# Splitting the last stage of an inverse FFT by residues modulo 3: three full matmuls and vector sums in place of four matmuls on 96 rows

## The chip, the cores and the metric

One Trainium2 chip, one of its cores. The metric is the device time of one execution in microseconds (us), lower is better.

## What is computed

Three parts follow one another on an input of 8 batches, 3072 tokens and 256 channels, all in 32-bit floats:

```python
X = np.fft.rfft(x, axis=1)
y = np.fft.irfft(X * (filt_r + 1j * filt_i), n=3072, axis=1)     # filter along the tokens
xk = mu_k * y + (1 - mu_k) * y_prev                              # y_prev: y one token earlier
xr = mu_r * y + (1 - mu_r) * y_prev
z = sigmoid(xr @ w_r) * (np.maximum(xk @ w_k, 0) ** 2 @ w_v)     # 256 -> 1024 -> 256
h = np.maximum(np.maximum(z @ w1, z @ w2), z @ w3)               # 256 -> 768
out = h @ w_out                                                  # 768 -> 256
```

## The kernel before, in words

The 3072 tokens of a batch are written as 96 x 32: token 32 p + m. The forward and the inverse FFT both run as matmuls with small tables. `fft` (L400) emits, per batch, the forward steps, the product with the filter and the first inverse step (`c_mm`, L506); its results go to a tensor in DRAM, `s2`, with the axes m (32), r (4 real components), g (24 frequency groups) and the channels. `fft_first` (L531) does the same for batch 0.

The second inverse step is the place of the change. A tile is four values of m (`MC`) with all 96 values of p, so 384 tokens; eight tiles make a batch, 64 make the run. `y_load` (L683) reads a tile's part of `s2` into `cin`, with the 96 pairs (r, g) on the partitions, by one DMA on SyncE's queue; the first tile of a batch also reads the last m into `cprev`. `y_mm` (L694) then does, for each half of the channels:

```python
for m in range(MC):
    mm(p[:, m], t[:, m, h * P : (h + 1) * P], wi_s[:, 0], m == 0, True, True)
...
nc.scalar.copy(yt[:, h, :, 1:], p[:, :MC].rearrange("c m t -> c t m"))
```

Each of the four matmuls has `cin` as the stationary operand (96 rows, 128 columns) and the 96 x 96 table `wi_s` as the moving one, in full 32-bit floats. ScalarE copies the 384 results out of PSUM into `yt`, where each p holds five tokens: the four of the tile and the one ahead of them, which GpSimd copies from the previous tile (L706), or ScalarE from `cprev` (L703). From `yt`, ScalarE (L714) and VectorE (L715) form the mixed input `xm`, and `split` (L249) makes a high part on ScalarE and a low part on GpSimd, `xh` and `xl`, once for r and once for k.

`r_mm`, `k_mm` and `v_mm` (L724, L734, L747) are the second part of the computation, with three matmuls for each product (high by high, high by low, low by high). A `v_mm` runs three `k_mm` later than the one whose result it uses (`LAG`, L208). `block` (L794), on pairs of tiles, is the third part, with `o_mm` (L865) behind it. Their weights `ws` are streamed from DRAM in the order of use, eight transfers ahead (`piece_of`, L333).

The order of the work is a list of units. For an even tile after the first ones, `y_mm` stands in the `kv` (L891) of the tile ahead of it, at its fifth `k_mm`; for an odd one, in `second` (L923), at the third block from its end. `drive` (L180) mixes the FFT of the next batch in between. A scheduler that works from estimated times then fixes the order on every engine, before the run; on the chip each engine's queue runs in that order.

Of the kernel before, what the change touches and what calls it, by code (L numbers as in the profile page):

```python
# [9 lines left out]
F32 = mybir.dt.float32  # L10
# [21 lines left out]
def fft_constants():  # L32


    n1 = np.arange(N1)
    n2 = np.arange(N2)
    wa = np.zeros((NP, 2, 2, NG))
    wi = np.zeros((2, 2, NG, NP))
    for j in range(2):
        for g in range(NG):  # L40
            ph = 2 * np.pi * ((n1 * g) % N1) / N1
            if g == 0:
                wa[j::2, 0, j, 0] = 1.0
                wa[j::2, 1, j, 0] = (-1.0) ** n1
                wi[0, j, 0, j::2] = 1.0 / N
                wi[1, j, 0, j::2] = (-1.0) ** n1 / N
            else:
                wa[j::2, 0, j, g] = np.cos(ph)
                wa[j::2, 1, j, g] = -np.sin(ph)
                wi[0, j, g, j::2] = 2 * np.cos(ph) / N  # L50
                wi[1, j, g, j::2] = -2 * np.sin(ph) / N
    wb = np.zeros((2, N2, NG, 2, N2))
    wc = np.zeros((2, N2, NG, 2, N2))
    freq = np.zeros((2, N2, NG), np.int64)
    for g in range(NG):
        for s in range(N2):
            if g:
                f = g + N1 * s
                th = 2 * np.pi * ((n2 * f) % N) / N
                c, sn = np.cos(th), np.sin(th)  # L60
                sg = 1.0 if s < NM else -1.0
                wb[0, :, g, 0, s] = c
                wb[1, :, g, 0, s] = sn
                wb[0, :, g, 1, s] = -sg * sn
                wb[1, :, g, 1, s] = sg * c
                wc[0, s, g, 0, :] = c
                wc[1, s, g, 0, :] = -sg * sn
                wc[0, s, g, 1, :] = sn
                wc[1, s, g, 1, :] = sg * c
                freq[:, s, g] = f if s < NM else N - f  # L70
            else:
                src = 0 if s < NM else 1
                f = N1 * s if s < NM else NG + N1 * (s - NM)
                th = 2 * np.pi * ((n2 * f) % N) / N
                c, sn = np.cos(th), np.sin(th)
                freq[:, s, g] = f
                if s == 0:
                    wb[0, :, 0, 0, 0] = 1.0
                    wb[0, :, 0, 1, 0] = (-1.0) ** n2
# [12 lines left out]
    return (
        wa.reshape(NP, NQ),
        wi.reshape(NQ, NP),
        wb.reshape(NK, NG, NK),
        wc.reshape(NK, NG, NK),
        freq.reshape(NK, NG),
    )


def radix3_constants():
# [62 lines left out]
    return w3, wb.reshape(NK, NG, NK)  # L164
# [33 lines left out]
def tile_spectral_moe(ctx: ExitStack, tc, x, xr, xz, filt, ones, wa, wa1, wi, wbc, wb1, wc1, filt1, filt0, mu, w_k, w_v, w_r, w1, w2, w3, w_out, out):  # L198
# [41 lines left out]
    wi_s = cpool.tile([NQ, 2, NP], F32, name="wi_s")  # L240
# [158 lines left out]

    def fft(b):  # L400
# [3 lines left out]
        s2 = dp.tile([NM, 4, NG, C], F32, tag="s2", name=f"s2_{b}")  # L404
        s2_of[b] = s2
# [100 lines left out]
        def c_mm(s):  # L506
# [6 lines left out]
            nc.scalar.dma_start(s2.rearrange("m r g c -> (m r) g c")[:, 2 * s : 2 * s + 2, :], o)  # L513
# [17 lines left out]
    def fft_first(pp, jobs):  # L531

        s1 = dp.tile([NM, 4, NG, C], F32, tag="s1", name="s1_0")
        s2 = dp.tile([NM, 4, NG, C], F32, tag="s2", name="s2_0")
        s2_of[0] = s2
# [96 lines left out]
        for s in range(NG // 2 + 2):  # L632
# [24 lines left out]
            if s >= 2:  # L657
# [6 lines left out]
                evac(s, p, s2.rearrange("m r g c -> (m r) g c")[:, 2 * s - 4 : 2 * s - 2, :], nc.scalar)  # L664
# [387 lines left out]
def layout(x, filt_r, filt_i, mu_k, mu_r, w_k, w_v, w_r, w1, w2, w3, w_out):  # L1052
    wa, wi, wb, wc, freq = fft_constants()
    C = x.shape[2]
    wa3, wb3 = radix3_constants()
    wah = np.stack(two_parts(wa3), axis=1)
    wis = np.zeros((NQ, 2, NP), np.float32)
    wis[:, 0] = wi
    wis[:, 1, 1:] = wi[:, :-1]
# [15 lines left out]
        "in_x": x[:1], "in_xr": xr, "in_xz": xz, "in_filt": filt, "in_ones": ones, "in_wa": wah, "in_wa1": wa.astype(np.float32), "in_wi": wis, "in_wbc": wbc, "in_wb1": wb.astype(np.float32), "in_wc1": wc.astype(np.float32),  # L1075
# [6 lines left out]
```

## Time and profile before

| | us |
|---|---|
| median of 3 runs (3162.06 to 3163.3) | 3162.99 |
| the profiled execution, its own time | 3161.27 |
| its span in the profile | 3159.5 |
| TensorE matmuls busy | 3080.0 (97%) |
| TensorE weight loads busy | 3020.4 (96%) |
| VectorE busy | 1922.4 (61%) |
| ScalarE busy | 1884.8 (60%) |
| GpSimd busy | 1858.6 (59%) |

The time of an execution is its span with a little around it, here 1.8 us. In the profile's views PE is TensorE's matmuls, PEld its weight loads, DVE is VectorE, ACT is ScalarE, POOL is GpSimd, SP is SyncE; a q behind a name is that engine's queue of DMA issues. A group of instructions is named output<-inputs. A 32-bit float matmul (`py`, `ps`) leaves two records in the trace, each with a weight load of its own; a matmul of the split kind (float32r) leaves one. Matmuls are pipelined: a record lasts longer than the time until the next one can start, so the cost of one in a row of many is read from start to start.

### The profile page before, as it was taken

To read this page: it belongs to the slowest core of one execution; us is meant where nothing else is said; L and a number is where in the kernel's file an instruction comes from. 1 tells how busy PE (TensorE), PEld (TensorE's weight loads), DVE (VectorE), ACT (ScalarE), POOL (GpSimd) and SP (SyncE) were. 2 spreads that over 40 slices of the span, in tenths; PEclk is the share of its full clock that TensorE was granted. 3 is DMA by queue.
4 is the path that set the end of the run, shared out by engine and by line. 5 is a ranking of instruction groups with operands and counts; after the bars stand their busy time and mean duration, and the time that the engine had idled before them with its cause. 6 is when DMAs were issued, how large, how long until landed. Compare 5 with 4: busy or idle time off the path is not lost.

```text
span 3159.5 us, 55818 instructions
## 1 busy us (share of the span) xinstructions
PE 3080.0 (97%) x19172; PEld 3020.4 (96%) x19172; DVE 1922.4 (61%) x3050; ACT 1884.8 (60%) x3968; POOL 1858.6 (59%) x1591
## 2 busy tenths in 40 slices
PE   6799999999999999999999999999999999999998
PEld 4699999999999999999999999999999999999998
DVE  4976676556664666556655566656666566555554
ACT  5556656566565566656666556566666566555554
POOL 3545765567554676556756566556765468444443
PEclk8899999999999999999999999999999999999999
DMA  9878787667776677758767587765887567555554
GB/s 298 267 260 285 235 305 227 188 197 251 260 233 184 224 240 227 254 171 259 251 221 220 183 263 261 227 205 183 262 268 237 180 214 232 178 169 165 161 170 122
DMA packets 400951, 705.92 MB, mean 223 GB/s; under 512 B 41472, under 2 KB 153120, under 8 KB 400032
## 3 DMA queue, kind: packets, MB, share of 16 engines
q1 hardware_dynamic: 333648, 621.26, 62.1%
q10 hardware_dynamic: 64576, 72.45, 6.5%
q0 software_dynamic: 2448, 8.65, 0.8%
q8 instruction: 155, 2.54, 0.3%
q14 instruction: 124, 1.02, 0.1%
HBM read 616.35 MB, written 92.14 MB: 224 GB/s over the span
## 4 chain that ended last, share of the span: by engine, by line
PE 81%; DVE 6%; DMA 5%; POOL 3%; issue 3%; ACT 1%; ACTq 0%; SPq 0%; POOLq 0%; DVEq 0%
PE pb L225 17%; PE pk L225 15%; PE pv L225 14%; PE po L225 12%; PE pe L225 8%; PE pa L225 5%; PE pr L225 4%; PE py L225 3%; DMA ws<-wud 3%; PE pc L225 2%; DVE sc L773 1%; POOL klo L251 1%; DMA s<-e 1%; DVE xd L427 1%; POOL hh L251 1%
## 5 line engine op out<-in xcount | busy, mean ns | idle before, releaser
L225 PE MATMUL pb<-x,ws 128*128 128x384 f32 x3456 | 751.7, 337 | 10.2 <-DMA ws<-wud 7.0
L251 POOL TENSOR_TENSOR hh<-m,hh 128x384 fp32r<-128x384 f32 x384 | 409.5, 1075 | 563.5 <-ACT hh L250 481.4
L251 POOL TENSOR_TENSOR klo<-kr,khi 128x384 fp32r<-128x384 f32 x492 | 520.8, 1064 | 233.2 <-ACT khi L250 205.1
L225 PEld LDWEIGHTS pb<-x,ws 128*128 128x128 f32 x3456 | 596.1, 188 | 20.5 <-issue 6.4
L741 DVE SCALAR_TENSOR_TENSOR kr<-pk,kr 128x384 f32<-128x384 f32 x512 | 281.4, 553 | 429.7 <-ACT kr L740 427.5
L225 PE MATMUL pv<-khi,ws 128*128 128x384 f32 x2048 | 481.3, 338 | 4.9 <-ACT khi L250 4.9
L225 PE MATMUL po<-wo_hi,hh 128*128 128x256 f32 x2304 | 481.4, 282 | 3.3 <-ACT hh L250 2.6
L250 ACT CAST khi<-kr 128x384 fp32r<-128x384 f32 x512 | 261.9, 513 | 226.8 <-DVE kr L741 191.9
L225 PEld LDWEIGHTS po<-wo_hi,hh 128*128 128x128 f32 x2304 | 391.1, 189 | 5.0 <-ACT hh L250 3.4
L225 PE MATMUL pe<-x,ws 128*128 128x384 f32 x1728 | 387.8, 338 | 3.5 <-DVE m L848 1.4
L225 PEld LDWEIGHTS pv<-khi,ws 128*128 128x128 f32 x2048 | 358.9, 188 | 8.5 <-ACT khi L250 6.4
L225 PE MATMUL pk<-xh,wk_hi 128*128 128x384 f32 x1024 | 341.2, 336 | 3.8 <-ACT xh L250 3.8
L225 PE MATMUL pk<-xl,wk_hi 128*128 128x384 f32 x1024 | 343.7, 336 | 0.9 <-DVE xl L251 0.9
L225 PE MATMUL pk<-xh,wk_lo 128*128 128x384 f32 x1024 | 343.3, 335 | 0.0
L225 PE MATMUL po<-wo_lo,hh 128*128 128x256 f32 x1152 | 316.8, 282 | 0.0
L740 ACT ACTIVATE kr<-pk 128x384 f32<-128x384 f32 x512 | 249.8, 489 | 108.8 <-POOL klo L251 56.8
L225 PEld LDWEIGHTS pe<-x,ws 128*128 128x128 f32 x1728 | 297.4, 188 | 8.8 <-DVE sc L855 3.1
L225 PE MATMUL pv<-klo,ws 128*128 128x384 f32 x1024 | 298.6, 338 | 2.4 <-DVE klo L251 1.3
L856 DVE TENSOR_TENSOR m<-sc,m 128x384 f32<-128x384 f32 x384 | 293.9, 768 | 8.4
L251 POOL TENSOR_TENSOR xl<-xm,xh 128x768 fp32r<-128x768 f32 x126 | 234.9, 1880 | 70.3 <-ACT xh L250 70.2
L250 ACT CAST hh<-m 128x384 fp32r<-128x384 f32 x384 | 192.6, 514 | 123.5 <-DVE m L856 85.6
L809 ACT COPY v<-pb 128x384 f32<-128x384 f32 x288 | 138.3, 480 | 188.8 <-PE pb L225 181.4
(134 smaller groups left out, 6143.1 us busy)
## 6 DMA issues: line engine op xcount, KB each, us to landing
ws<-wud SPq DMA_DIRECT2D x864, 256.0 KB, 3.8
ws<-wvd SPq DMA_DIRECT2D x512, 256.0 KB, 3.7
wbc<-wbcd SPq DMA_DIRECT2D x84, 512.0 KB, 5.5
filt<-in_filt SPq DMA_DIRECT2D x84, 512.0 KB, 4.3
ws<-wud SPq DMA_DIRECT2D x288, 128.0 KB, 3.7
xz<-in_xz SPq DMA_DIRECT2D x56, 512.0 KB, 5.2
cin<-s SPq DMA_DIRECT2D x64, 384.0 KB, 4.1
out_dram<-osb ACTq DMA_DIRECT2D x192, 128.0 KB, 2.9
```

What stands on the lines that cost most here:

```text
L225: nc.tensor.matmul(o, lhsT=wgt, rhs=rhs, start=start, stop=stop, skip_group_check=more)
L250: nc.scalar.copy(hi, src)
L251: (lo_eng or nc.gpsimd).tensor_tensor(lo, src, hi.bitcast(F32), ALU.subtract)
L427: nc.vector.tensor_tensor(v, z[:, 0], z[:, 1], ALU.subtract)
L740: nc.scalar.activation(r, p, AF.Relu)
L741: nc.vector.scalar_tensor_tensor(r, p, 0.0, r, ALU.max, ALU.mult)
L773: eng.tensor_tensor(t, a, b, ALU.subtract)
L809: nc.scalar.copy(st[to], st[of])
L856: nc.vector.tensor_tensor(m, c, m, ALU.max)
```

## The change

An output at p is a sum over the 24 frequency groups. The groups whose number is divisible by 3 (8 of them) give the same at p, p + 32 and p + 64, that is 1024 tokens apart; call it A. The other 16 give B0, B1 and B2 there, and B0 + B1 + B2 = 0. So the three outputs are A + B0, A + B1 and A - B0 - B1.

`s2` becomes two DRAM tensors, `s2a` with the 8 groups and `s2b` with the 16. `cin` has 128 partitions: one slice of `s2a` with all four m (4 x 4 x 8 rows) and two of `s2b` with two m each (2 x 4 x 16 rows). The table holds a block for each m. One matmul of 128 columns forms A for the four m, two more form B0 and B1 for two m each. ScalarE copies A to `y0`, and VectorE makes the three outputs from `y0` and PSUM. `y_load` issues two DMAs in place of one (four in place of two where `cprev` is read). The tables of the first inverse step are reordered to fit; its matmuls are as many and as large as before.

```diff
     wa_s = cpool.tile([NK, 2, 2, NK], F32R, name="wa_s")
-    wi_s = cpool.tile([NQ, 2, NP], F32, name="wi_s")
+    wi_s = cpool.tile([NK, 2, NK], F32, name="wi_s")
+    wie_s = cpool.tile([NQ, NP], F32, name="wie_s")
...
+    def s2_tiles(b):
+        s2_of[b] = [dp.tile([NM, 4, n, C], F32, tag=f"s2{k}", name=f"s2{k}_{b}") for k, n in (("a", GA), ("b", GB))]
...
     def y_load(i):
         b, q = divmod(i, NCH)
-        s2v = s2_of[b].rearrange("m r g c -> (r g) m c")
-        t = mp.tile([NQ, MC, C], F32, tag="cin", name="cin", bufs=1)
-        nc.sync.dma_start(t, s2v[:, q * MC : (q + 1) * MC, :])
+        sa, sb = s2_of[b]
+        ms = slice(q * MC, (q + 1) * MC)
+        t = mp.tile([NK, 3, C], F32, tag="cin", name="cin", bufs=1)
+        nc.sync.dma_start(t[:, 0], sa[ms].rearrange("m r g c -> (m r g) c"))
+        nc.sync.dma_start(t[:, 1:], sb[ms].rearrange("(k m) r g c -> (m r g) k c", k=2))
         e = None
         if q == 0:
             e = mp.tile([NQ, C], F32, tag="cprev", name="cprev", bufs=1)
-            nc.sync.dma_start(e, s2v[:, NM - 1, :])
+            nc.sync.dma_start(e[: 4 * GA], sa[NM - 1].rearrange("r g c -> (r g) c"))
+            nc.sync.dma_start(e[4 * GA :], sb[NM - 1].rearrange("r g c -> (r g) c"))
         cs["c", i] = t, e
 
     def y_mm(i):
...
         for h in range(2):
-            p = ps.tile([P, MC + 1, NP], F32, tag="pm", name="py")
-            for m in range(MC):
-                mm(p[:, m], t[:, m, h * P : (h + 1) * P], wi_s[:, 0], m == 0, True, True)
+            p = ps.tile([P, (MC + 1) * NP], F32, tag="pm", name="py")
+            pv = p[:, : MC * NP].rearrange("c (k m n) -> c k m n", k=NR, m=MC)
+            hs = slice(h * P, (h + 1) * P)
+            mm(pv[:, 0], t[:, 0, hs], wi_s[:, 0], True, True, True)
+            for k in range(2):
+                mm(pv[:, 1:, 2 * k : 2 * k + 2], t[:, 1 + k, hs], wi_s[:, 1], False, True, True)
             if e is not None:
-                mm(p[:, MC], e[:, h * P : (h + 1) * P], wi_s[:, 1], False, True, True)
-                nc.scalar.copy(yt[:, h, :, 0], p[:, MC])
-            nc.scalar.copy(yt[:, h, :, 1:], p[:, :MC].rearrange("c m t -> c t m"))
+                mm(p[:, MC * NP :], e[:, hs], wie_s, False, True, True)
+                nc.scalar.copy(yt[:, h, :, 0], p[:, MC * NP :])
+            y0 = mp.tile([P, MC, NS], F32, tag="y0", name="y0")
+            nc.scalar.copy(y0, pv[:, 0])
+            yv = yt[:, h, :, 1:].rearrange("c (k n) m -> c k m n", k=NR)
+            two, twice = bass.broadcast_tensor_aps(pv[:, 1:], y0.rearrange("c (k m) n -> c k m n", k=1))
+            nc.vector.tensor_tensor(yv[:, :2], two, twice, ALU.add)
+            nc.vector.tensor_tensor(y0, y0, pv[:, 1], ALU.subtract)
+            nc.vector.tensor_tensor(yv[:, 2], y0, pv[:, 2], ALU.subtract)
```

The line numbers of the changed kernel are some 16 to 40 higher: L225 (the matmul helper) becomes L241, L704 (the copy out of PSUM) becomes L734, L714 and L715 (`xm`) become L749 and L750, and the three sums are L737, L738 and L739.

The scheduler's order shows what stands in the queues. On TensorE, at `y_mm` of tile 34 (an even tile, without `cprev`), before:

```order
L225 MATMUL pa<-xah,wa_s 128x512
L225 MATMUL py<-wi_s,cin 128x96 x8
L225 MATMUL pv<-khi,ws 128x384 x2
L225 MATMUL pv<-klo,ws 128x384
L225 MATMUL pv<-khi,ws 128x384 x2
```

and now:

```order
L241 MATMUL pa<-xah,wa_s 128x512
L241 MATMUL py<-wi_s,cin 128x128
L241 MATMUL py<-wi_s,cin 128x2x64 x2
L241 MATMUL pv<-khi,ws 128x384
L241 MATMUL py<-wi_s,cin 128x128
L241 MATMUL py<-wi_s,cin 128x2x64 x2
L241 MATMUL pv<-khi,ws 128x384
L241 MATMUL pv<-klo,ws 128x384
```

Eight matmuls in a row have become three, one matmul of `v_mm`, and three more; what stands ahead and behind is the same.

On ScalarE at the same tile, before (the first row copies out of PSUM for one half of the channels, `xm` is the first step of the mix, `kr` and `khi` belong to `k_mm` of the tile ahead, `yh` to the FFT):

```order
L704 COPY yt<-py 128x96x4
L714 ACTIVATE xm<-yt,mu_s 128x384 x2
L250 CAST khi<-kr 128x384
L704 COPY yt<-py 128x96x4
L250 CAST yh<-filt 128x512
L714 ACTIVATE xm<-yt,mu_s 128x384 x2
L740 ACTIVATE kr<-pk 128x384
```

and now (`osb` is an output tile):

```order
L734 COPY y_21234<-py 128x128
L734 COPY y_21243<-py 128x128
L775 ACTIVATE kr<-pk 128x384
L917 COPY osb<-po 128x512
L749 ACTIVATE xm<-yt,mu_s 128x384 x4
L922 DMA out_dram<-osb 32x4x256
L268 CAST khi<-kr 128x384
```

The four `xm` stood right behind ScalarE's own copies; now they stand behind two copies of 128, and need VectorE's sums, with two other instructions between.

On VectorE at the same tile, before:

```order
L856 TENSOR_TENSOR m<-sc,m 128x384
L741 SCALAR_TENSOR_TENSOR kr<-pk,kr 128x384 x4
L715 SCALAR_TENSOR_TENSOR xm<-yt,nmu_s,xm 128x384 x4
L741 SCALAR_TENSOR_TENSOR kr<-pk,kr 128x384 x6
```

and now:

```order
L891 TENSOR_TENSOR m<-sc,m 128x384
L776 SCALAR_TENSOR_TENSOR kr<-pk,kr 128x384 x4
L737 TENSOR_TENSOR yt<-py,y_21234 128x2x4x32
L737 TENSOR_TENSOR yt<-py,y_21243 128x2x4x32
L738 TENSOR_TENSOR y_21234<-y_21234,py 128x128
L738 TENSOR_TENSOR y_21243<-y_21243,py 128x128
L739 TENSOR_TENSOR yt<-y_21234,py 128x4x32
L739 TENSOR_TENSOR yt<-y_21243,py 128x4x32
L776 SCALAR_TENSOR_TENSOR kr<-pk,kr 128x384
L750 SCALAR_TENSOR_TENSOR xm<-yt,nmu_s,xm 128x384 x4
```

Six sums have come in ahead of the `xm` of VectorE, the two halves of the channels in turn.

## Rows read from the trace of the kernel before

**Rows 1.** Busy time in stretches of the span: PE, PEld, DVE, ACT, POOL, then clock and DMA.

```profile
0.00:110.00 110.00, 66.35 (x212) 43.68 (x212) 60.52 (x83) 51.68 (x86) 50.26 (x48) 0.80 0.89 289
110.00:240.00 130.00, 122.89 (x776) 119.44 (x776) 103.03 (x163) 74.45 (x151) 59.85 (x52) 0.97 0.80 266
820.00:1210.00 390.00, 387.06 (x2442) 382.12 (x2442) 240.96 (x383) 239.08 (x507) 240.87 (x204) 1.00 0.71 228
1600.00:2000.00 400.00, 398.10 (x2513) 393.56 (x2512) 241.52 (x388) 245.97 (x522) 247.10 (x212) 1.00 0.71 228
```

**Rows 2.** Waits of PE: who waited for whom, total us, times, longest us.

```profile
PE pb L225 <- DMA ws<-wud: 7.0, 12, 1.2
PE pv L225 <- ACT khi L250: 4.9, 6, 1.8
```

**Rows 3.** The tile py: count, duration ns min/median/max, first and last start, form.

```profile
L225 PEld LDWEIGHTS py<-wi_s,cin x1024: 187/192/334, 99.8 to 3064.0; 96*128 96x128 f32 x171
L225 PE MATMUL py<-wi_s,cin x1024: 245/275/498, 99.8 to 3064.0; 96*128 96x96 f32 x171
```

**Rows 4.** The tile ps, same columns: 32-bit float matmuls of 128 columns.

```profile
L225 PEld LDWEIGHTS ps<-wf,eye x252: 187/192/333, 127.0 to 227.5; 128*128 128x128 f32 x126
L225 PE MATMUL ps<-wf,eye x252: 270/275/418, 127.2 to 227.6; 128*128 128x128 f32 x126
```

**Rows 5.** Timeline of PE at one py group: start us, us, instruction, count.

```profile
923.48 0.68 PE L225 MATMUL pb<-x,ws 128*128 128x384 f32 x3
924.00 1.92 PE L225 MATMUL py<-wi_s,cin 96*128 96x96 f32 x16
925.71 0.77 PE L225 MATMUL pb<-x,ws 128*128 128x384 f32 x3
926.31 0.28 PE L225 MATMUL po<-wo_hi,hh 128*128 128x256 f32 x1
```

**Rows 6.** Timeline of PE at one ps group.

```profile
142.79 3.29 PE L225 MATMUL ps<-wf,eye 128*128 128x128 f32 x28
145.83 0.42 PE L225 MATMUL pk<-xh,wk_hi 128*128 128x384 f32 x1
146.09 0.34 PE L225 MATMUL pk<-xl,wk_hi 128*128 128x384 f32 x1
146.26 0.34 PE L225 MATMUL pk<-xh,wk_lo 128*128 128x384 f32 x1
```

**Rows 7.** Groups of VectorE with a source in PSUM: count, busy us, mean ns, idle before.

```profile
L852 DVE TENSOR_TENSOR m<-pb,m 128x384 f32<-128x384 f32 x192 | 106.2, 553 | 107.5 <-PE pb L225 107.0
L499 DVE TENSOR_TENSOR filt<-pb,filt 128x512 f32<-128x512 f32 x84 | 58.1, 692 | 2.4
```

**Rows 8.** Groups of ScalarE that copy py out of PSUM.

```profile
L704 ACT COPY yt<-py 128x384 f32<-128x384 f32 x128 | 61.1, 485 | 39.9 <-PE py L225 39.8
L703 ACT COPY yt<-py 128x96 f32<-128x96 f32 x16 | 5.4, 335 | 2.2 <-PE py L225 2.2
```

**Rows 9.** The issue of cin on SyncE's queue, from the view of its line.

```profile
L687 SPq DMA_DIRECT2D cin<-s x64: 320/321/1593, 91.2 to 3004.8; - x64
```

**Rows 10.** Timelines of PE, ACT and POOL from y_mm to r_mm of an even tile.

```profile
1613.47 0.59 PE L225 MATMUL pv<-khi,ws 128*128 128x384 f32 x2
...
1614.24 0.54 ACT L704 COPY yt<-py 128x384 f32<-128x384 f32 x1
1614.68 2.13 ACT L714 ACTIVATE xm<-yt,mu_s 128x384 f32<-128x384 f32 x4
1616.72 0.47 ACT L740 ACTIVATE kr<-pk 128x384 f32<-128x384 f32 x1
1617.09 0.57 ACT L882 COPY osb<-po 128x512 f32<-128x512 f32 x1
...
1618.48 3.64 POOL L251 TENSOR_TENSOR xl<-xm,xh 128x768 fp32r<-128x768 f32 x2 [3.04 <-ACT xh L250]
...
1622.93 0.34 PE L225 MATMUL pr<-xl,wr_hi 128*128 128x384 f32 x1
```

More of the change, by code (lines that the diff above doesn't have):

```diff
@@ L132, in radix3_constants @@
     w3 = np.stack([wa0.reshape(NK, NK), wa12.reshape(NK, NK)], axis=1)
+    p = np.arange(NP)
+    wf = np.zeros((4, NG, NP))
+    for a, g in enumerate(ORDER):
+        for r, f in ((0, g), (2, N1 - g)) if g else ((2, NG),):
+            ph = 2 * np.pi * (f * p % NP) / NP
+            wf[r, a] = 2 * np.cos(ph) / N
+            wf[r + 1, a] = -2 * np.sin(ph) / N
+        if not g:
+            wf[0, a] = 1.0 / N
+            wf[1, a] = (-1.0) ** p / N
+    wi0 = np.zeros((j4, 4, GA, j4, NS))
+    wi12 = np.zeros((j2, 4, GB, 2, j2, NS))
+    for j in range(j4):
+        wi0[j, :, :, j] = wf[:, :GA, :NS]
+    for j in range(j2):
+        wi12[j, :, :, :, j] = wf[:, GA:, : 2 * NS].reshape(4, GB, 2, NS)
+    wi3 = np.stack([wi0.reshape(NK, NK), wi12.reshape(NK, NK)], axis=1)
+    wie = np.zeros((NQ, NP))
+    wie[:, 1:] = np.concatenate([wf[:, :GA].reshape(-1, NP), wf[:, GA:].reshape(-1, NP)])[:, :-1]
     m = np.arange(NM)
     wb = np.zeros((NM, 4, NG, 2, N2))
+    wc = np.zeros((2, N2, NG, NM, 4))
     for a, g in enumerate(ORDER):
@@ L147, in radix3_constants @@
                 wb[:, r + 1, a, 1, s] = sg * cj * c
+                wc[0, s, a, :, r] = c
+                wc[1, s, a, :, r] = -sg * sn
+                wc[0, s, a, :, r + 1] = cj * sn
+                wc[1, s, a, :, r + 1] = sg * cj * c
             elif s == 0:
@@ L150, in radix3_constants @@
                 wb[:, 0, a, 1, 0] = (-1.0) ** m
+                wc[0, 0, a, :, 0] = 1.0
+                wc[1, 0, a, :, 0] = (-1.0) ** m
             else:
@@ L157, in radix3_constants @@
                     wb[:, s % 2, a, 1, s] = -sn
+                    wc[0, s, a, :, s % 2] = 2 * c
+                    wc[1, s, a, :, s % 2] = -2 * sn
                 else:
@@ L163, in radix3_constants @@
                     wb[:, 3, a, 1, s] = cj * c
-    return w3, wb.reshape(NK, NG, NK)
+                    wc[0, s, a, :, 2] = c
+                    wc[1, s, a, :, 2] = -sn
+                    wc[0, s, a, :, 3] = cj * sn
+                    wc[1, s, a, :, 3] = cj * c
+    return w3, wb.reshape(NK, NG, NK), wc.reshape(NK, NG, NK), wi3, wie
 def as_float(bits):
@@ L197, in tile_spectral_moe @@
 @with_exitstack
-def tile_spectral_moe(ctx: ExitStack, tc, x, xr, xz, filt, ones, wa, wa1, wi, wbc, wb1, wc1, filt1, filt0, mu, w_k, w_v, w_r, w1, w2, w3, w_out, out):
+def tile_spectral_moe(ctx: ExitStack, tc, x, xr, xz, filt, ones, wa, wa1, wi, wie, wbc, wb1, wc1, filt1, filt0, mu, w_k, w_v, w_r, w1, w2, w3, w_out, out):
     nc = tc.nc
@@ L245, in load_small @@
         nc.scalar.dma_start(wi_s, wi)
+        nc.scalar.dma_start(wie_s, wie)
         nc.scalar.dma_start(mu_s, mu)
@@ L398, in tile_spectral_moe, with s2_part @@
     wbc_d = [dp.tile([NK, 4, 2, NK], F32R, tag=f"wbcd{s}", name=f"wbcd{s}", bufs=1) for s in range(NG // 2)]
+    def s2_tiles(b):
+        s2_of[b] = [dp.tile([NM, 4, n, C], F32, tag=f"s2{k}", name=f"s2{k}_{b}") for k, n in (("a", GA), ("b", GB))]
+    def s2_part(b, s):
+        t, k = (s2_of[b][0], 2 * s) if 2 * s < GA else (s2_of[b][1], 2 * s - GA)
+        return t.rearrange("m r g c -> (m r) g c")[:, k : k + 2, :]
     def fft(b):
@@ L403, in fft @@
         s1b = dp.tile([NM, 4, GB, C], F32, tag="s1b", name=f"s1b_{b}")
-        s2 = dp.tile([NM, 4, NG, C], F32, tag="s2", name=f"s2_{b}")
-        s2_of[b] = s2
+        s2_tiles(b)
         st = {}
@@ L512, in c_mm @@
             nc.scalar.copy(o, p)
-            nc.scalar.dma_start(s2.rearrange("m r g c -> (m r) g c")[:, 2 * s : 2 * s + 2, :], o)
+            nc.scalar.dma_start(s2_part(b, s), o)
         for s in range(NBS + 2):
@@ L533, in fft_first @@
         s1 = dp.tile([NM, 4, NG, C], F32, tag="s1", name="s1_0")
-        s2 = dp.tile([NM, 4, NG, C], F32, tag="s2", name="s2_0")
-        s2_of[0] = s2
+        s2_tiles(0)
         xv = x[0].rearrange("(p m) c -> p m c", m=NM)
@@ L663, in fft_first @@
                     mm(p[:, k], wt[g // LW][2][:, g % LW], q[:, k], False, True)
-                evac(s, p, s2.rearrange("m r g c -> (m r) g c")[:, 2 * s - 4 : 2 * s - 2, :], nc.scalar)
+                evac(s, p, s2_part(0, s - 2), nc.scalar)
             if s in CONV:
@@ L1052, in layout @@
 def layout(x, filt_r, filt_i, mu_k, mu_r, w_k, w_v, w_r, w1, w2, w3, w_out):
-    wa, wi, wb, wc, freq = fft_constants()
+    wa, wb, freq = fft_constants()
     C = x.shape[2]
-    wa3, wb3 = radix3_constants()
+    wa3, wb3, wc, wi3, wie = radix3_constants()
     wah = np.stack(two_parts(wa3), axis=1)
-    wis = np.zeros((NQ, 2, NP), np.float32)
-    wis[:, 0] = wi
-    wis[:, 1, 1:] = wi[:, :-1]
     wbc = np.stack(two_parts(wb3) + two_parts(wc), axis=1)
@@ L1074, in layout @@
     arrays = {
-        "in_x": x[:1], "in_xr": xr, "in_xz": xz, "in_filt": filt, "in_ones": ones, "in_wa": wah, "in_wa1": wa.astype(np.float32), "in_wi": wis, "in_wbc": wbc, "in_wb1": wb.astype(np.float32), "in_wc1": wc.astype(np.float32),
+        "in_x": x[:1], "in_xr": xr, "in_xz": xz, "in_filt": filt, "in_ones": ones, "in_wa": wah, "in_wa1": wa.astype(np.float32), "in_wi": wi3.astype(np.float32), "in_wie": wie.astype(np.float32), "in_wbc": wbc, "in_wb1": wb.astype(np.float32), "in_wc1": wc.astype(np.float32),
         "in_filt1": filt1, "in_filt0": filt0, "in_mu": mu,
```

19 lines of the change are left out of this document (1 added, 18 removed).

## The prediction

> **What bounds the kernel now.** I read the table of busy time by stretches first, since a share over the whole run would mix a start-up with a steady state. In the two stretches of the middle [rows 1] TensorE's matmuls are busy for 387.06 of 390 us and 398.10 of 400 us, at a granted clock of 1.00, while VectorE, ScalarE and GpSimd stand at 240 to 247 us, some 62%. TensorE is the bound there, and the others have more than a third of their time free. Only the first 110 us are different: TensorE is busy for 66.35 us at a clock of 0.80. From 110 to 240 us VectorE is at 103.03 of 130 us, its fullest stretch.
>
> The waits of TensorE come next. Its two largest waits of the steady part are 7.0 us for weight transfers and 4.9 us for ScalarE's `khi`, summed over the whole run [rows 2]. So a microsecond taken from TensorE's own work is a microsecond of the span, as long as nothing new makes it wait. What remains is to price the matmuls taken out, and to look for new waits.
>
> **TensorE, the term that carries the forecast.** There are 64 tiles, two halves of the channels each, and four matmuls per half: 512 matmuls, and 1024 records, two for each [rows 3]. The change makes three per half: 384 matmuls, 768 records. The 16 matmuls on `cprev` stay.
>
> What does one record cost? The record itself lasts 275 ns at 96 columns, and 275 ns at 128 columns too [rows 3, 4], with a weight load of 192 ns at both. That speaks for equal prices, but it is the duration in the pipeline. So I read from start to start. A group of 16 records of 96 columns takes 925.71 - 924.00 = 1.71 us, and the three matmuls behind it take 926.31 - 925.71 = 0.60 us where such a three takes 924.00 - 923.48 = 0.52 us, so 0.08 us more belongs to the group [rows 5]. That is 1.79 / 16 = 0.112 us a record. A group of 28 records of 128 columns takes 145.83 - 142.79 = 3.04 us, and the matmul behind it 0.26 us in place of 0.17, so 3.13 / 28 = 0.112 us [rows 6]. At this size a record costs the same at 96 and at 128 columns: each needs a full weight load, and the columns that stream by are not what it waits for. The gain is (1024 - 768) x 0.112 = **28.7 us**. As a bound from above this also serves, since nothing else is taken from TensorE. The bound from below is a price that goes with columns: 4 x 96 = 3 x 128, so nothing would be gained. I take the upper one, because the `ps` rows are the same kind of matmul with exactly the new width.
>
> A rule of the Trainium skill speaks against it. "TensorE: Matmul & The Clock Gate", section "Back-to-back issue gap", gives a gap of N / 2.4 + 2.5 ns for N columns at the full clock: 42.5 ns at 96 and 55.8 ns at 128. By that, 1024 records would be 43.5 us and 768 would be 42.9 us, a gain of 0.6 us in place of 28.7. The trace's 112 ns at both widths disagrees with it for this kind of matmul.
>
> The printed order splits the two halves of this tile by one matmul of `v_mm`. Other tiles were split before: over the whole order there are 89 groups of `py` before and 90 now, so for the 0.08 us that a group leaves behind I add nothing.
>
> **VectorE.** Three sums per half are added, 128 times: one of 256 elements and two of 128, each with a source in PSUM. The nearest rows are 553 ns at 384 elements and 692 ns at 512 [rows 7], so 1.09 ns an element and 0.136 us ahead of them: about 0.414 us at 256 and 0.275 us at 128. Estimated from these, a half costs 0.414 + 2 x 0.275 = 0.96 us, the run 123 us. VectorE's mean goes from 61 to 65%. That it writes `yt` with a stride of five could cost more; ScalarE's copy with the same stride takes 485 ns [rows 8]. Beside TensorE's 97% all of this is covered, on average.
>
> **ScalarE.** A copy of 384 (485 ns) becomes one of 128. Between 335 ns at 96 and 485 ns at 384 [rows 8], that is about 0.35 us, so 128 x 0.13 = 17 us less. It is off the path, worth nothing by itself.
>
> **The chain from `py` to the next tile's matmuls.** Before, TensorE is through with `py` at 1613.47, ScalarE's last copy ends at 1614.24 + 0.54 = 1614.78, 1.3 us later [rows 10]. Now the last half needs its copy (0.35 us) and, as the order prints them, 0.41 + 4 x 0.275 = 1.5 us of sums: 1.9 us, and with two more handoffs some 2 to 2.7. The chain grows by 0.7 to 1.4 us. Who waits for it? GpSimd makes the first `xl` from 1618.48 for half of 3.64 us, until 1620.30, and TensorE wants it at 1622.93 [rows 10]. That leaves 2.6 us, so `r_mm` should not be late. For odd tiles there are three more blocks in between.
>
> **A new wait on ScalarE.** This is the price I am least sure of. ScalarE's four `xm` must wait for VectorE, and its queue runs in order: `khi` and the copies of other work stand behind. The order puts two instructions in between, of 0.47 and 0.57 us [rows 10], against some 1.5 us of VectorE's sums. So ScalarE stands for half a microsecond to one in each tile, and `khi` is late by as much; `v_mm` needs it through GpSimd. The cover is `LAG`, three `k_mm` and two `v_mm` of TensorE's time, some 5 us, of which the chain from `kr` to `klo` takes about three. Today all waits of `pv` for `khi` come to 4.9 us [rows 2], 0.08 us a tile. I bound the new ones by nothing and by half a microsecond a tile, 32 us, and take **4 us**, the size of today's, which is the nearest row.
>
> **DMA.** The bytes are the same. SyncE issues 72 more transfers, 0.32 us each [rows 9]: 23 us on a queue, ahead of weights fetched eight transfers early. TensorE's whole wait for these weights is 7.0 us [rows 2]; I add nothing, and one more microsecond or two if that cover is thin.
>
> **Start-up.** The first `py` run at the low clock, so four matmuls fewer give back up to a microsecond, and VectorE, then at its fullest [rows 1], takes it again for the sums. I set it to zero, within 2 us.
>
> **The sum.** -28.7 + 4 = -24.7 us. Against the profiled execution's own 3161.27 us that gives 3136.6 us. The median of the runs shown is 1.7 us above that execution, so the forecast for a median is **3138 us**, 0.8% faster. What a measurement of this kernel can tell from no change is about 0.2%, 6 us.
>
> **Rivals.**
> (1) *Columns set the price.* If a record costs by its columns, TensorE gains 0.6 us or nothing, the new wait of 4 us stays, and the time is 3163 + 4 = about 3166 us, no change by the 0.2%. For it: three times 128 is four times 96. Against it: equal starts and equal records at both widths [rows 3 to 6], though the `ps` group was read early in the run. The rule of the Trainium skill named above would give this outcome.
> (2) *Part of it is lost in waits.* The wait on ScalarE costs TensorE 0.2 us a tile, 13 us: 3163 - 28.7 + 13 = 3147 us. For it: `pv` waits for `khi` already, so that cover is not thick.
> (3) *ScalarE's wait becomes the bound at every tile.* `khi` and the copies out of PSUM are held back until TensorE stands. It decides from 28.7 / 64 = 0.45 us a tile. At 0.75 us, the middle of ScalarE's estimated standing time, it is 48 us: 3163 - 28.7 + 48 = 3182 us, slower. For it: a round trip through VectorE where ScalarE had its own result. Against it: ScalarE is only 60% busy, `v_mm` runs three `k_mm` late, and the 2.6 us at `r_mm`.
>
> **Chances.** The forecast, 3130 to 3142 us: 0.70. Rival 2, 3142 to 3156: 0.14. Rival 1, within 6 us of no change: 0.08. Rival 3: 0.08. So faster by over 0.2%: 0.84; within: 0.08; slower: 0.08. The range reaches from 3130 (the whole 28.7 us without a wait and a few us of luck in the order) to 3156 us, the end of rival 2, which leaves out 0.16.
>
> **What would show it.** In the profile of the changed kernel: 768 records of `py` with `cin`, at 0.11 us from start to start; TensorE's busy time less by some 28 us; VectorE up by 120 us and ScalarE down by 17; sums of 0.41 and 0.28 us. `pv` waiting for `khi` should stay below 10 us. The forecast is wrong if a `py` group of six takes 0.8 us rather than 0.6 to 0.7, or if TensorE's waits for `khi`, `klo` or `xl` grow to tens of microseconds.

## The result: slower, and the profile after

The changed kernel takes 3179.93 us (median of 6 runs, 3176.46 to 3185.41) against 3162.72 us for the kernel before beside it (3161.36 to 3165.59): ratio 1.0056, 95% interval 1.0043 to 1.0069. That is 17 us slower where 25 us faster was forecast.

First the busy time on the page of the changed kernel, for the execution of 3185.39 us:

```profile
PE 3075.9 (97%) x18916; PEld 2994.8 (94%) x18916; DVE 2033.8 (64%) x3434; ACT 1869.8 (59%) x3968; POOL 1863.8 (59%) x1591
```

TensorE has 256 records fewer, as said. VectorE gained 111 us and ScalarE lost 15. Next the tile `py` and ScalarE's copy out of it, with the columns of [rows 3], and the three sums of VectorE, with the columns of [rows 7]:

```profile
L241 PEld LDWEIGHTS py<-wi_s,cin x768: 187/192/333, 98.6 to 3087.6; 128*128 128x128 f32 x192
L241 PE MATMUL py<-wi_s,cin x768: 270/275/552, 98.6 to 3087.8; 128*128 128x128 f32 x192
L734 ACT COPY y<-py x128: 254/266/359, 102.1 to 3088.5; 128x128 f32<-128x128 f32 x128
```

```profile
L737 DVE TENSOR_TENSOR yt<-py,y 128x256 f32<-128x256 f32 x128 | 77.3, 639 | 14.9 <-ACT y L734 12.4 <-PE py L241 2.4
L739 DVE TENSOR_TENSOR yt<-y,py 128x128 f32<-128x128 f32 x128 | 46.2, 397 | 1.2
L738 DVE TENSOR_TENSOR y<-y,py 128x128 f32<-128x128 f32 x128 | 33.8, 282 | 1.0
```

A half's sums take 639 + 282 + 397 ns = 1.32 us; 0.96 were forecast.

Did TensorE get its time back? From 240 us on, added up from start to start over the timeline, `py` with `cin` goes from 960 records and 100.6 us to 720 records and 74.0 us: **26.6 us saved**, at 0.105 us a record of 96 columns and 0.103 us a record of 128. The term that carried the forecast is in the trace. The Trainium skill ("TensorE: Matmul & The Clock Gate", "Back-to-back issue gap") gives the 55.8 ns at 128 columns for an isolated matmul, and about 81 ns for a stream of weight loads and matmuls. So its section does not hold that formula against a stream, as the prediction did; a record of these 32-bit matmuls took 103 ns, more than either figure.

So the time was lost elsewhere. The stretches after the start-up, before and then after (columns of [rows 1]):

```profile
240.00:3140.00 2900.00, 2879.53 (x18122) 2847.06 (x18123) 1753.46 (x2795) 1754.19 (x3725) 1744.31 (x1488) 1.00 0.69 220
```

```profile
240.00:3140.00 2900.00, 2853.10 (x17720) 2799.53 (x17719) 1846.30 (x3131) 1730.51 (x3699) 1740.74 (x1481) 1.00 0.68 219
```

In the same 2900 us, the weight loads (PEld) are busy 47.5 us less, and other engines remain near 60%. TensorE does not have less to do by 47 us; it stands still more. Its idle time in front of weight loads from 240 us on, added up over the timeline, is 43.7 us before and 88.8 us after: 45 more. And 45 - 26.6 = 18 us, most of the loss: the two profiled executions (3161.27 and 3185.39 us) lie 24 us apart, the medians 17.

Much of the other 6 us is TensorE's clock. In the stretches below the granted clock (the last column but two, a mean in which 1.00 is 2.4 GHz and 0.50 is 1.2 GHz) was for a while at its lower level, 1.2 GHz; for the rest of the time from 240 to 3140 us it was at 2.4 GHz. Before, there is one such stretch, then after, there are four:

```profile
455.00:466.00 11.00, 8.98 (x45) 8.35 (x45) 9.04 (x11) 5.43 (x13) 9.62 (x7) 0.84 0.99 336
```

```profile
274.00:281.00 7.00, 5.34 (x21) 5.07 (x21) 4.06 (x7) 4.58 (x10) 5.06 (x5) 0.76 0.89 280
458.00:469.00 11.00, 7.60 (x32) 7.53 (x32) 9.01 (x11) 5.06 (x11) 9.30 (x7) 0.69 0.76 254
513.00:520.00 7.00, 6.11 (x23) 5.50 (x24) 2.26 (x3) 4.32 (x10) 4.54 (x5) 0.76 0.41 103
1892.00:1899.00 7.00, 6.18 (x28) 6.21 (x29) 4.69 (x8) 2.99 (x7) 5.23 (x6) 0.76 0.46 134
```

By these columns that is 3.5 us at the lower level before and 17 us after. At each of these places TensorE had just stood still; at the last one for 1.87 us, and a microsecond later its matmuls start 0.32 us apart where it was 0.17:

```profile
1892.82 0.76 PE L241 MATMUL pe<-x,ws 128*128 128x384 f32 x3 [1.87 <-issue]
1893.42 0.33 PE L241 MATMUL pr<-xh,wr_hi 128*128 128x384 f32 x1
1893.59 0.37 PE L241 MATMUL pr<-xl,wr_hi 128*128 128x384 f32 x1
...
1894.08 0.52 PE L241 MATMUL pr<-xh,wr_hi 128*128 128x384 f32 x1
1894.40 0.52 PE L241 MATMUL pr<-xl,wr_hi 128*128 128x384 f32 x1
```

Estimated from these rows, 13.5 us more at the lower level cost some 6 us. So a wait can cost more than its own length. The chain that ended last shows the standing still as well, before and then after:

```profile
PE 81%; DVE 6%; DMA 5%; POOL 3%; issue 3%; ACT 1%; ACTq 0%; SPq 0%; POOLq 0%; DVEq 0%
```

```profile
PE 66%; POOL 6%; DMA 6%; DVE 5%; issue 3%; ACT 2%; ACTq 0%; POOLq 0%; DVEq 0%; SPq 0%
```

Where does it stand still? The waits of the weight loads (who waited for whom, total us, times, longest), before and after:

```profile
PEld pv L225 <- POOL klo L251: 6.5, 18, 0.5
PEld pv L225 <- ACT khi L250: 6.4, 6, 2.0
PEld pb L225 <- DVE m L852: 3.6, 4, 1.1
```

```profile
PEld pv L241 <- ACT khi L268: 21.4, 26, 3.8
PEld pb L241 <- DVE m L887: 8.1, 10, 1.1
PEld pr L241 <- DVE m L887: 5.9, 10, 0.6
PEld pv L241 <- POOL klo L269: 3.6, 8, 0.6
PEld pr L241 <- POOL xl L269: 2.3, 5, 0.7
PEld pr L241 <- ACT xh L268: 2.2, 4, 1.0
```

These are waits of the whole run. From 240 us on, the wait for `khi` was next to nothing before:

```profile
PEld pv L225 <- ACT khi L250: 0.5, 1, 0.5
```

```profile
PEld pv L241 <- ACT khi L268: 14.6, 21, 1.1
```

The direct victims of the sums, `pr` waiting for `xh` and `xl`, lose 4.5 us. Most is lost far from `y_mm`. Of the 45 us, added up from 240 us on over all tiles that wait, `khi`, the cast of `k_mm`, has 14, `m`, in the blocks, has 12 (19.9 for 7.9), and 9 have no releaser in the profile ("issue"). The diff leaves those instructions as they were, though `m` and VectorE's part of `kr`, which `khi` reads, stand in the queue that the sums have joined. What also touches them is the order: on TensorE alone the orders of the two kernels differ in over a thousand places.

Three theories went to the chip. **S**: the sums delay each tile by themselves. **D**: `cin` in two transfers delays the weights. **Q**: the scheduler, with other estimated times, made another order of the whole program, and that order costs by itself.

### The profile page after: what moved, and what is told of

Same layout as the page of the kernel before. It is cut to its first block, busy times and chain, and to the rows that moved or that the text cites. A ratio compares the mean times of both kernels' runs of the same rounds, so it can differ in the third digit from the quotient of the medians.

```text
span 3183.2 us, 55838 instructions
## 1 busy us (share of the span) xinstructions
PE 3075.9 (97%) x18916; PEld 2994.8 (94%) x18916; DVE 2033.8 (64%) x3434; ACT 1869.8 (59%) x3968; POOL 1863.8 (59%) x1591
## 4 chain that ended last, share of the span: by engine, by line
PE 66%; POOL 6%; DMA 6%; DVE 5%; issue 3%; ACT 2%; ACTq 0%; POOLq 0%; DVEq 0%; SPq 0%
PE pb L241 15%; PE pk L241 12%; PE po L241 11%; PE pv L241 10%; PE pe L241 7%; PE pa L241 4%; PE pr L241 4%; DMA ws<-wud 3%; POOL klo L269 2%; PE py L241 2%; PE pc L241 1%; DVE m L891 1%; DMA xr<-in_xr 1%; POOL x L269 1%; DMA xz<-in_xz 1%
## 5 line engine op out<-in xcount | busy, mean ns | idle before, releaser
L241 PE MATMUL pb<-x,ws 128*128 128x384 f32 x3456 | 755.1, 338 | 17.8 <-DMA ws<-wud 12.3
L269 POOL TENSOR_TENSOR hh<-m,hh 128x384 fp32r<-128x384 f32 x384 | 417.5, 1095 | 556.9 <-ACT hh L268 465.6
L241 PEld LDWEIGHTS pb<-x,ws 128*128 128x128 f32 x3456 | 596.6, 189 | 33.8 <-issue 12.1
L241 PE MATMUL po<-wo_hi,hh 128*128 128x256 f32 x2304 | 484.6, 282 | 4.5 <-ACT hh L268 3.8
L241 PE MATMUL pv<-khi,ws 128*128 128x384 f32 x2048 | 475.4, 339 | 13.6 <-ACT khi L268 13.0
L241 PEld LDWEIGHTS po<-wo_hi,hh 128*128 128x128 f32 x2304 | 390.5, 189 | 7.1 <-ACT hh L268 4.8
L241 PE MATMUL pe<-x,ws 128*128 128x384 f32 x1728 | 388.7, 339 | 6.2 <-issue 1.9
L241 PEld LDWEIGHTS pv<-khi,ws 128*128 128x128 f32 x2048 | 357.7, 188 | 22.5 <-ACT khi L268 21.4
L241 PE MATMUL pk<-xh,wk_hi 128*128 128x384 f32 x1024 | 338.9, 338 | 7.8 <-ACT xh L268 6.2
L241 PE MATMUL pk<-xl,wk_hi 128*128 128x384 f32 x1024 | 343.8, 336 | 0.4 <-DVE xl L269 0.4
L241 PE MATMUL pk<-xh,wk_lo 128*128 128x384 f32 x1024 | 343.2, 335 | 0.0
L891 DVE TENSOR_TENSOR m<-sc,m 128x384 f32<-128x384 f32 x384 | 320.9, 839 | 9.0
L241 PE MATMUL po<-wo_lo,hh 128*128 128x256 f32 x1152 | 316.7, 281 | 0.0
L241 PEld LDWEIGHTS pe<-x,ws 128*128 128x128 f32 x1728 | 299.2, 189 | 13.1 <-DVE sc L890 3.9
L241 PE MATMUL pv<-klo,ws 128*128 128x384 f32 x1024 | 289.4, 337 | 2.0 <-DVE klo L269 0.8
L241 PEld LDWEIGHTS po<-wo_lo,hh 128*128 128x128 f32 x1152 | 218.0, 189 | 0.4
```

The source lines that it names most:

```text
L241: nc.tensor.matmul(o, lhsT=wgt, rhs=rhs, start=start, stop=stop, skip_group_check=more)
L269: (lo_eng or nc.gpsimd).tensor_tensor(lo, src, hi.bitcast(F32), ALU.subtract)
L891: nc.vector.tensor_tensor(m, c, m, ALU.max)
```

## The experiments

**Leaving out the sums.** `e1_no_sums` replaces `y0` and the sums; `e2_sums_unread` adds three VectorE sums on the same PSUM that nobody reads, with a constant for `y0`.

```diff
-            y0 = mp.tile([P, MC, NS], F32, tag="y0", name="y0")
-            nc.scalar.copy(y0, pv[:, 0])
...
+            nc.scalar.copy(yv, pv)
```

> Left out: the three sums; ScalarE copies the 384 results of the three matmuls out of PSUM in one instruction, as the kernel before does. Theory S (the sums on VectorE, and ScalarE's wait for them, cost TensorE some 50 us of stalls): the 27 us of matmuls show undisturbed, about 3136 us. Theory Q (the scheduler's new order of all queues costs it, wherever it differs): the order differs here too, so anything from 3130 to 3160. Theory D (cin in two transfers delays the weights): no faster than the kernel before, 3163 us or more.

> As e1, and VectorE also does three sums of the same shapes out of PSUM, into a tile that nobody reads (its other operand is a constant). Nobody waits for the sums except the PSUM bank. If VectorE's time and the bank are what costs: near the changed kernel, 3170 to 3185 us. If it is ScalarE's wait for the sums and the longer chain to xl: near e1, within 5 us of it.

Measured: e1 3166.27 us, ratio 1.0004 (0.9995 to 1.0014); e2 3180.2 us, 1.0049 (1.0032 to 1.0065). S misses: without any sum, with the same 26.6 us saved on `py`, nothing is gained. Q's range, 3130 to 3160, is missed as well, and D's, 3163 or more, is met. e2 lies where its expectation puts VectorE's time and the PSUM bank as what costs. But e2 has an order of its own, too, and no run has its sums in the order of e1, so this does not tell them apart; e3, next, speaks against VectorE's time. One flaw came to light in e1's trace, and it holds for every kernel without sums below: its one ScalarE copy is dear.

```profile
L734 ACT COPY yt<-py 128x384 f32<-128x384 f32 x128 | 111.6, 906 | 33.1 <-PE py L241 33.1
```

That is 906 ns for the 485 of [rows 8], so a tile's chain is 0.42 us a half longer in them than in the kernel before.

**Faster sums.** `e3_m_inner` lays `y0` and the PSUM reads out with m innermost, so that VectorE writes `yt` in runs of four.

```diff
-            yv = yt[:, h, :, 1:].rearrange("c (k n) m -> c k m n", k=NR)
+            yv = yt[:, h, :, 1:].rearrange("c (k n) m -> c k n m", k=NR)
```

> The changed kernel with the loops of the copy and of the sums exchanged, so that they write runs of four neighbours into yt in place of single elements five apart. If the step of the writes is what makes the sums 639 and 397 ns, they become about 414 and 280 ns, 45 us of VectorE less, and by theory S the time falls by 10 to 20 us, to 3160 to 3170 us. If reading PSUM with a step costs as much as writing with one, or by theory Q, no such fall: 3175 to 3185 us.

Measured: 3181.83 us, 1.0052 (1.0035 to 1.0069), no gain. The edit did what it should, since the first sum falls from 639 to 416 ns:

```profile
L738 DVE TENSOR_TENSOR yt<-py,y 128x256 f32<-128x256 f32 x128 | 51.0, 416 | 16.0 <-ACT y L735 13.6 <-PE py L241 2.4
```

**Another order alone.** Only the weight of `y_mm` in the unit list changes (1.3 to 1.0), which moves instructions but changes none: in the kernel before, in the changed one, and in e1.

> The kernel before, with the weight of y_mm in the list of units 1.0 in place of 1.3: the same instructions, and pieces of the FFT begin some units earlier or later in the order. Theory S: no effect, 3161 to 3165 us. Theory Q: an order alone can move the time by 5 us or more.

> The changed kernel with the weight of y_mm 1.0 in place of 1.3 in the unit list, as its three matmuls would suggest: the same instructions, other order. Theory Q: the order is a draw of some us either way, so the time differs from 3180 by 3 to 15 us in one direction or the other. Theory S: 3180 within 3 us, for the sums and the chain from py to xl are the same.

> The kernel without sums, with y_mm's weight 1.0 in place of 1.3 in the unit list: another order of the same instructions (values wrong for leaving out the sums). Theory Q (each order is a draw, before's was a good one): anywhere from 3148 to 3175, differing by some us from the 3166 of the same kernel at 1.3. If orders near each other cost alike: 3166 within 2 us.

Measured: 3171.69 us, 1.0024 (1.0014 to 1.0033), so 7.5 us for an order alone; 3179.52, 1.0052 (1.0039 to 1.0065), as before the edit, where S expected it and Q did not; 3171.22, 1.0034 (1.0022 to 1.0046), 9 us more than e1. An order by itself is worth up to some 10 us here, and the scheduler's estimate does not tell which is the better one.

**Pinned orders.** This tells Q apart directly. After tracing, each engine's instructions are chained in a given order, by edges that set the issue order and wait for nothing:

```diff
+        for d in steps:
+            at += d + 1
+            i = mine[at]
+            if last is not None:
+                tc.add_manual_dep(i, last.name, mybir.DependencyInfo(mybir.DependencyClass.NoSync, mybir.DependencyReason.DATA), reason="order")
+            last = i
```

> The changed kernel, instruction for instruction, but every engine and queue issues in the order that it had in the kernel before (three matmuls stand where four stood, the second transfer of a tile and the VectorE sums are placed by the scheduler). Theory Q (the order that the scheduler made for the new program costs what the matmuls save; before at 3163): about 3140 us, that is 27 us less from the matmuls, plus a few us for the sums' own delay; a ratio near 0.993. Theory S (the sums on VectorE cost it by themselves, each tile's xh and xl come too late): no better than the changed kernel, 3175 to 3185 us. Theory D (the transfers in two parts): 3175 to 3185 us as well.

> The kernel without sums (three matmuls of 128 columns, one ScalarE copy, values wrong for leaving out the sums), with every engine issuing in the order of the kernel before. Theory Q: the whole 27 us show, 3136 us (3133 to 3141). Theory D (the weights and the tile's cin come late because a tile is now two transfers and the sequence is stored in two tensors): it stays where it stood with its own order, 3164 us. The difference to the run before it (same order, with sums) is what the sums cost by themselves: theory S expects 14 us or more, theory Q under 8.

> The mirror: the instructions of the kernel before, four matmuls and no sums, in the order that the scheduler made for the changed kernel. Theory Q: slower than before by tens of us, 3180 to 3205, since the matmuls' 27 us are added to an order that is already worse. Theories S and D: like the kernel before within some us, 3160 to 3172.

> The kernel without sums (three matmuls, one ScalarE copy of 384 columns, values wrong for leaving out the sums) in the order that the scheduler made for the changed kernel. Theory Q (order): the 27 us of the matmuls off the 3195 us of the kernel before in that same order, 3168 us; the changed kernel's 3180 us then hold some 12 us of the sums themselves. Theory S (the sums' delay is the whole loss, the order is harmless): 3151 us or less, like the same kernel in the order of before.

> The changed kernel in the order of the kernel before, but the tile's chain from py to xh and xl (ScalarE's y0, xm and xh, the VectorE sums and xm, POOL's yt and xl) is left to the scheduler, so that ScalarE need not stand still in front of the sums. If the 92 us of the earlier forced order were that standing still (168 us of waits on ScalarE): 3152 to 3170 us, under the changed kernel's 3180. If the later xh and xl stop TensorE anyway: 3180 to 3257.

Ratios to the kernel before, with 95% intervals:

| instructions of | order of before | order of the changed kernel |
|---|---|---|
| the kernel before | 1 | 1.0099 (1.0085 to 1.0112) |
| without sums | 0.9959 (0.9948 to 0.9971) | 1.0073 (1.0060 to 1.0085) |
| the changed kernel, all pinned | 1.0297 (1.0284 to 1.0310) | 1.0056 (1.0043 to 1.0069) |
| the changed kernel, chain free | 1.0066 (1.0053 to 1.0079) | |

Read the right column first. The kernel before, not one instruction changed, loses 0.99%, 31 us, by the new order, and it has the waits of the changed kernel without any sum:

```profile
PEld pv L255 <- ACT khi L280: 17.4, 25, 3.5
PEld pb L255 <- DVE m L882: 7.6, 9, 1.2
PEld pr L255 <- DVE m L882: 5.9, 10, 0.6
```

In that order the changed instructions then win 14 us (1.0056 for 1.0099). Read this way, **the loss is the order's**: +31 - 14 = +17. Without the sums that order is no faster (1.0073). Such a kernel has the dear copy of e1 in place of the sums, so this shows no cost of the sums there, but does not exclude one. Q's 3180 to 3205 for the kernel before is met, its 3168 us for the one without sums was missed at 3186.58.

Now the left column, which says what the sums do to the old order. Without sums it gives 13 us, half of what Q expected. With them, pinned, it loses 94, which Q's 3140 us misses altogether: ScalarE stands in front of `xm`. In that kernel, and then in the changed one:

```profile
ACT xm L779 <- DVE yt L769: 168.2, 93, 5.0
```

```profile
ACT xm L749 <- DVE yt L739: 27.5, 34, 1.3
```

The scheduler of the changed kernel put other work ahead of `xm`. How the 168 us reach TensorE is not shown in full: of its 143 us of idle time in front of weight loads in f1, from 240 us on, 60 have no releaser in the profile. With only the tile's chain left free (h2), the loss is still 21 us. The sums fit into no order that was tried without a price.

So the table has two readings. Order first, it is +31 for the order and -14 for the instructions; instructions first, +94 and then -77 for the order. Neither alone is the cause: the sums do not fit the old order, and the order that the scheduler made with them in it costs 31 us by itself. The pair that comes nearest to a price of the order alone is the kernel without sums: the same instructions take 1.0004 in the order that the scheduler made for them (e1) and 0.9959 in the old one (f2), 14 us. An order made for other instructions may also cost by not fitting; that part of the 31 and the 94 us was not told apart.

**Asking for the tile earlier** (`f == 3` for 4, block `nb - 4` for `nb - 3`) gives the chain more room.

> The changed kernel with y_mm asked for one unit earlier in the unit list (f == 3 in place of 4, block nb-4 in place of nb-3), the scheduler free. Theory S (xh and xl late by the sums): under 3170 us, for the chain gets 2 to 10 us more. Theory Q (a new order that costs by itself): 3170 to 3195, no systematic gain.

Measured: 3195.86 us, 1.0106 (1.0093 to 1.0119), slower still: S misses again, and Q's upper end is passed by 1 us.

**What in the new order costs.** ScalarE's timeline of the changed kernel, some 30 us behind `y_mm` of tile 32, the tile of [rows 10] (start us, us, instruction, idle before it):

```profile
1652.12 0.51 ACT L268 CAST khi<-kr 128x384 fp32r<-128x384 f32 x1 [1.81 <-DVE kr L776]
1652.54 0.48 ACT L775 ACTIVATE kr<-pk 128x384 f32<-128x384 f32 x1
1653.75 0.49 ACT L775 ACTIVATE kr<-pk 128x384 f32<-128x384 f32 x1 [0.73 <-POOL klo L269]
1654.14 0.50 ACT L268 CAST khi<-kr 128x384 fp32r<-128x384 f32 x1
```

The same place in the kernel before:

```profile
1641.30 0.51 ACT L250 CAST khi<-kr 128x384 fp32r<-128x384 f32 x1 [2.50 <-DVE kr L741]
1641.72 0.48 ACT L740 ACTIVATE kr<-pk 128x384 f32<-128x384 f32 x1
1642.83 0.51 ACT L250 CAST khi<-kr 128x384 fp32r<-128x384 f32 x1 [0.62 <-DVE kr L741]
1643.25 0.48 ACT L740 ACTIVATE kr<-pk 128x384 f32<-128x384 f32 x1
```

After, the next group's `kr` stands ahead of a `khi`, and it must wait 0.73 us for GpSimd to be through with a buffer (`kr` has two). The cast behind it comes 1654.14 - 1652.12 = 2.02 us after the one before, in place of 1.53. Its input was ready at 1653.06 + 0.56 = 1653.62, half a microsecond earlier:

```profile
1653.06 0.56 DVE L776 SCALAR_TENSOR_TENSOR kr<-pk,kr 128x384 f32<-128x384 f32 x1 [0.97 <-ACT kr L775]
```

TensorE feels it at once, in its own timeline:

```profile
1654.70 0.97 PE L241 MATMUL pv<-khi,ws 128*128 128x384 f32 x4 [0.30 <-ACT khi L268]
```

The Trainium skill names the ground in "PSUM — Partial Sum Buffer", "Engine vs sequencer instructions": ScalarE's queue is strictly first in, first out. The rows agree: a ready cast waits behind a `kr` that is not. The kernel before in the new order has this very piece, with the same idle time:

```profile
1656.10 0.48 ACT L770 ACTIVATE kr<-pk 128x384 f32<-128x384 f32 x1
1657.32 0.49 ACT L770 ACTIVATE kr<-pk 128x384 f32<-128x384 f32 x1 [0.74 <-POOL klo L281]
1657.71 0.50 ACT L280 CAST khi<-kr 128x384 fp32r<-128x384 f32 x1
```

In the orders of ScalarE, `kr` stands ahead of the group's earlier `khi` in 67 places of 512 before and in 129 after. Theory **K** says that these places are what the new order costs. One rule takes them out:

```diff
-        nc.scalar.activation(r, p, AF.Relu)
+        a = nc.scalar.activation(r, p, AF.Relu)
+        if i >= 4 and "khi" in cs:
+            tc.add_manual_dep(a.ins, cs["khi"], mybir.DependencyInfo(mybir.DependencyClass.NoSync, mybir.DependencyReason.DATA), reason="kr behind khi")
```

> The changed kernel with one rule for ScalarE's queue: from tile 4 on each relu kr is issued behind the cast khi of the channel group before it (10 places with kr ahead of the earlier khi are left, of 129). Theory K (these places are the cost of the new order, some 0.7 us each over the 67 of the kernel before): 3140 to 3165 us. Rival (they only go along with a bad order): 3172 to 3188.

> The kernel without sums (values wrong for leaving them out) with the same rule on ScalarE's queue (10 such places left of 112). Theory K: the matmuls' 27 us show at last, 3130 to 3150 us. Rival: 3160 to 3175, as without the rule.

> The kernel before with the same rule (10 such places left of 67). Theory K: faster than before, 3145 to 3160. Rival: a new draw of the order, 3160 to 3180.

> The changed kernel with m innermost (its first VectorE sum 0.42 us in place of 0.64) and the same rule. Theory K: like the changed kernel with the rule, or up to 8 us faster if the sums' time now counts: 3135 to 3165. Rival: 3172 to 3188.

Measured: the changed kernel 3168.66 us, 1.0020 (1.0011 to 1.0029); without sums 3162.05, 1.0000 (0.9991 to 1.0009); the kernel before 3162.31, 1.0000 (0.9991 to 1.0009); with m innermost 3167.1, 1.0015 (1.0006 to 1.0024). So the changed kernel with the rule loses 6 us in place of 17, and the kernel before gains nothing. The wait of the whole run and, second, that from 240 us on is now:

```profile
PEld pv L241 <- ACT khi L268: 11.3, 12, 3.1
PEld pv L241 <- ACT khi L268: 4.8, 6, 0.8
```

The wait that K named has gone down, from 14.6 to 4.8 us. But none of the four times lies in K's range: 3168.66 and 3167.1 fall between K and its rival, 3162.05 and 3162.31 in the rival's. The kernel without sums had 112 such places and gains 1 us, so their number is no price. And the rule makes the scheduler write another order everywhere: waits for `m`, which it does not name, fell as well, from 19.9 to 10.7 us. How much of the 11 us is due to these places, and how much to another order, is not shown. Idle time in front of weight loads is still 74.6 us in i1, 69.8 in i2 and 49.7 in i3, spread over `klo`, `m`, `gate` and the issue of instructions, the largest single wait 13 us.

**The rest of the 27 us.** Even in the old order, the kernel without sums shows 13 of 27. Two kernels in that order:

```diff
+            if e is None:
+                mm(p[:, MC], t[:, MC - 1, h * P : (h + 1) * P], wi_s[:, 0], False, True, True)
```

```diff
-        nc.sync.dma_start(t, s2v[:, q * MC : (q + 1) * MC, :])
+        nc.sync.dma_start(t[:, :2], s2v[:, q * MC : q * MC + 2, :])
+        nc.sync.dma_start(t[:, 2:], s2v[:, q * MC + 2 : (q + 1) * MC, :])
```

> The kernel before with a fifth matmul of 96 columns (the fourth again, into 96 columns that nobody reads) in each half of the 56 tiles that have no earlier column: 112 matmuls of two records more, every engine in the order of the kernel before. At 0.112 us a record it adds 25 us if TensorE is the bound there: 3188 us (3183 to 3193). If waits of other engines hide part of it, as they seem to hold back part of the saving: 3170 to 3182.

> The kernel before with each tile's cin loaded in two transfers of half the size, one behind the other, every engine otherwise in the order of the kernel before. Theory D (the second transfer on SP's queue delays the weights): 3170 to 3177 us, the 12 to 14 us that the kernel without sums misses in that order. Otherwise: 3163 within 3 us.

Measured: j1 3193.27 us, 1.0096 (1.0082 to 1.0109); j2 3161.59 us, 1.0001 (0.9991 to 1.0010). D falls: a second transfer a tile costs nothing (that the sequence lies in two DRAM tensors is not in j2). And 224 records more cost 30 us, the whole of their price of 25 and a little over: upward, TensorE is the bound. Downward, half was seen; the rest is idle time, 58.6 us in front of weight loads in f2 for 43.7. Whether it went into the dear copy of those kernels or into other engines' chains was not told apart.

## Why the prediction was wrong

**The step that failed** is in its second paragraph: "a microsecond taken from TensorE's own work is a microsecond of the span, as long as nothing new makes it wait". All new waits together were priced at one term, +4 us for `khi`; they measured +45 us of idle time in front of weight loads, against 26.6 us saved. New waits were looked for only beside `y_mm`, in the order at one tile; for the rest the old order was taken to stand ("I add nothing" for the 90 groups of `py` in place of 89). In its place the runs showed that the change comes with a new order of every queue, which costs 31 us even with the instructions of the kernel before, in waits for `khi` and `m`, tens of microseconds away from the tile.

The cover was misread, too: the 4.9 us of `pv` waiting for `khi` [rows 2], which the prediction counts to the steady part, lie ahead of 240 us but for 0.2. In the steady part there was no such wait to take as the nearest row.

Point by point:

- *TensorE's 28.7 us*: right. 26.6 us from start to start for 60 of the 64 tiles, at 0.103 to 0.105 us a record in place of 0.112; the price does not go by columns, so rival 1 is out.
- *The sums, 0.96 us a half*: 1.32. Two terms were mis-sized: 0.414 was 0.639 and one 0.275 was 0.397, both for sums that write `yt` with a stride of five; the one that does not, 0.282, was right, and e3's 416 and 280 ns show that the stride was the reason. The copy of 485 ns that the prediction set beside them has no such stride: it writes runs of four. No effect of it on the time was seen (e3 beside the changed kernel, i4 beside i1).
- *ScalarE's new wait, 4 us*: the stop named there, waits of `pv` for `khi` under 10 us, was passed: 13.0 us on PE, against 4.9 [rows 2]. From 240 us on the weight loads waited 14.6 us, under the bound of 32. The cause was not only the one named: ScalarE stood 27.5 us in front of `xm`, about 0.4 us a tile, but the same order without sums (g1) has 12.7 us of this wait. (ScalarE's order of the kernel before, shown ahead of the prediction, is in the trace that of tile 38 and not of tile 34, where both copies come first and then the four `xm`.)
- *Rival 3*, 3182 us with a chance of 0.08, gave nearly the time, by luck. Its mechanism is seen where the old order is pinned (f1), not in the changed kernel, whose scheduler had moved away from it.
- *The chain to `r_mm`*: 4.5 us of waits for `xh` and `xl` appeared. Small.
- *DMA 0*: right by j2. `pb` waits 12.3 us for `ws` in place of 7.0, but the kernel before in the new order has 10.1, with one transfer a tile.

What stays open is the last 6 us (1.0020 with the rule), what the sums cost by themselves in the new order, and the 14 of 27 us that f2 misses. No version that has the sums in it beat the kernel before.

## What to carry to other kernels

Where a scheduler writes the order from estimated times, a change has two prices: that of its instructions and that of the new order. Pinning the order of either kernel on the other's instructions shows both, and whether they can be had apart; here they could not. In the new order, look for a queue where an instruction that waits for a buffer stands ahead of one that is ready: with one rule against it the changed kernel lost 6 us in place of 17, though the rule changed the order elsewhere, too.

## What was not expected of the hardware

A VectorE sum of 256 elements takes 639 ns when it writes them one by one, five apart (the changed kernel), and 416 ns when it writes runs of four (e3). ScalarE's copy of 384 columns from PSUM into the same tile takes 485 ns in runs of four [rows 8] and 906 ns one by one (e1). A difference in the last dimension of a write was worth up to a factor of 1.9.
